# Where the first stores of batched V go, and in which order the first segment adds up its output

## The chip, the cores and the metric

The kernel runs on one core of a Trainium2 chip. The metric is device time in microseconds (us) of one execution. The core's engines have these names in the profile: PE is TensorE (matmuls; its weight loads are PEld), DVE is VectorE, ACT is ScalarE, POOL is GpSimd, SP is SyncE, which mostly starts transfers. L712 is line 712 of the kernel in question, so the same statement has another number in another kernel: the output sums (Wo) are L701 in the kernel before, L712 in the changed one, and L714 in experiments that add two lines.

## The reference, cut to what matters

```python
for s in range(n_seg):                      # 64 segments of 32 rows
    xs = x[:, s*32:(s+1)*32, :]
    h = concatenate([mem, xs])              # 8 memory rows + 32 rows, 512 wide
    q, k, v = h @ Wq, h @ Wk, h @ Wv        # 32 heads of 128
    p = softmax(mask(q @ k.T * scale))
    o = (p @ v) @ Wo                        # back to 512
    mem = o[:, :8, :]                       # what the next segment needs
    outs.append(o[:, 8:, :])
# ... then a residual, a layer norm and a gated feed-forward part
```

The segments are a chain: segment 1 cannot project its memory rows before segment 0's output has been summed over all heads. At the start the four weight matrices (4 MB each) also have to come in, and Wo is the last of them.

## The kernel before

The last 8 of each segment's 32 rows are taken out of the chain: their Q, K and V are computed in batches of 16 segments (128 rows), ahead of the segments that use them; this is "batched V". Batch ck = 0 covers segments 0 to 15. Its V tiles n = 0 to 7 are scaled into SBUF and go to device memory by GpSimd; the first four tiles of ck = 1 follow on the SyncE queue behind Wo:

```python
def vx_evac(ck, n, bank, eng="act", q="sp"):
    if ck == 1 and n < 4:
        t, tok = (hbuf, xo)[n // 2][:, n % 2, :], ...
    elif ck == 0:
        t, tok = part[:, n, :], ...
    else:
        t, tok = Vs[:, 0, :], [("Vs", 0)]
    # ... PSUM -> t on ACT or DVE
    if q is not None:
        em.add(q, lambda e: e.dma_start(dst, ...), reads=tok, writes=[("vext", ck, n)], dma=True)
    return lambda: sp(lambda e: e.dma_start(dst, ...), ...)
# ...
for n in range(8):
    # ...
    start_v(0, n)                 # store at once, by GpSimd
    if n % 2 == 1:
        start_v(1, n // 2)        # its store is kept in `stores`
# ...
for hq in range(4):
    load_wo(hq)                   # 4 x 1 MB
# ... batched K; V loads of segments 0 and 1
for f in stores:
    f()
```

At the end of each segment, Wo is summed for one half of the 512 columns, then for the other. The first half's memory columns (`mem_out`) are what the next segment's first projection waits for:

```python
Wo(WOQ, OB, 0, OC)                # 32 matmuls, first half, all quarters of Wo
part_evac(s, OB, 0, OC)           # ACT
Wo(WOQ[:6], OB2, OC, D)           # 24 of the second half
if s + 1 < NSEG:
    mem_out(s, 0)                 # PE, then the copy into hT on DVE
    mask_dve()
Wo(WOQ[6:], OB2, OC, D)           # the last 8
```

The softmax here doesn't subtract the row's maximum and nothing guards it: scores larger than these inputs give would overflow.

Of the kernel before, what the change touches and what calls it, by code (L numbers as in the profile page):

```python
# [178 lines left out]
def fast_path(nc, st, keep, A_x, A_mem0, A_Wq, A_Wk, A_Wv, A_Wo, A_seg_len, B_w_in, B_w_sp, B_b_sp, B_w_out, out):  # L179
    S = A_x.shape[1]  # L180
    D = A_x.shape[2]
# [13 lines left out]
    CK = 16  # L195
# [9 lines left out]
    em = Emitter(n_dma_sems=40)  # L205

    def sb(name, shape, dt):
        return st.enter_context(nc.sbuf_tensor("f_" + name, shape, dt))
# [11 lines left out]
    w_o = region(3 * WSZ, WSZ).rearrange("p (h d) -> p h d", h=H)  # L220
# [14 lines left out]
    NVX = 3  # L235
    Vx = sb("Vx", [128, NVX, 2, 128], BF)
    Vs = sb("Vs", [128, 2, 512], BF)
# [3 lines left out]
    part = sb("part", [128, 8, 512], BF)  # L241
    partx = sb("partx", [128, 512], BF)
    xn = sb("xn", [128, 2, 512], BF)
    hbuf = sb("hbuf", [128, 2, 512], BF)
    xo = sb("xo", [128, 2, 512], BF)
    wst = sb("wst", [128, RB, 64], BF)
    ident = sb("ident", [128, 128], BF)
    mask = sb("mask", [128, 448], BF)
    ones = sb("ones", [128, 128], BF)
# [20 lines left out]
    wT_d = nc.dram_tensor("wT_d", [S // 64, 128, RB, 64], BF, kind="Internal").ap()  # L270

    ps = st.enter_context(nc.psum_tensor("f_ps", [128, 8, 512], F32))
# [8 lines left out]
    def sp(fn, **k):  # L281
        return em.add("sp", fn, dma=True, **k)
# [217 lines left out]
                   reads=[("hTe", ck % 3, dc // 2), ("W", 2, n // 2)], writes=[PB(bank)])  # L500

    def vx_evac(ck, n, bank, eng="act", q="sp"):
        if ck == 1 and n < 4:
            t, tok = (hbuf, xo)[n // 2][:, n % 2, :], [(("h", "xo")[n // 2], n % 2)]
        elif ck == 0:
            t, tok = part[:, n, :], [("part", n, 0), ("part", n, 1)]
        else:
            t, tok = Vs[:, 0, :], [("Vs", 0)]
        if eng == "act":
            act(lambda e: e.activation(out=t, in_=ps[:, bank, :], func=ACT.Copy, scale=VSC), reads=[PB(bank)], writes=tok)  # L510
        else:
            dve(lambda e: e.tensor_scalar(out=t, in0=ps[:, bank, :], scalar1=VSC, scalar2=None, op0=ALU.mult), reads=[PB(bank)], writes=tok)
        dst = vext_d[ck, n // 4, 2 * (n % 4):2 * (n % 4) + 2, :, :].rearrange("g p f -> p g f")
        if q is not None:
            em.add(q, lambda e: e.dma_start(dst, t.rearrange("p (g f) -> p g f", g=2)), reads=tok, writes=[("vext", ck, n)], dma=True)
        return lambda: sp(lambda e: e.dma_start(dst, t.rearrange("p (g f) -> p g f", g=2)), reads=tok, writes=[("vext", ck, n)])

    def load_vx(s, q="sp"):
        i = s % CK
        for b in range(2):  # L520
            src = vext_d[s // CK, b, :, 8 * i:8 * i + 8, :].rearrange("g k (r e) -> g (k r) e", r=2)
            em.add(q, lambda e, b=b, src=src: e.dma_start(Vx[:, s % NVX, b, :], src),
                   reads=[("vext", s // CK, n) for n in range(4 * b, 4 * b + 4)], writes=[("Vx", s % NVX, b)], dma=True)



# [6 lines left out]
    OB = 2  # L533
# [3 lines left out]
    OB2 = 6  # L537
    FBK = 7
    OC = 256
# [151 lines left out]
    cTh = cT[:].rearrange("p c (b g q) -> p (c b g) q", b=2, q=40)  # L691


    WOQ = ((0, 0), (2, 0), (0, 1), (2, 1), (1, 0), (3, 0), (1, 1), (3, 1))

    def Wo(cbs, bank, d0, d1):
        for c, b in cbs:
            for g in range(4):
                h = 16 * b + 4 * c + g
                i = 8 * c + 4 * b + g  # L700
                pe(lambda e, h=h, g=g, i=i, b=b, c=c: e.matmul(  # L701
                    ps[32 * g:32 * g + 32, bank, 0:d1 - d0], lhsT=cTh[:, i, 8:40], rhs=w_o[:, h, d0:d1], start=((c, b) == WOQ[0]),
                    stop=((c, b) == WOQ[-1]), tile_position=(0, 32 * g)),
                    reads=[("cT", c, b), ("Wo", h // 8)], writes=[PB(bank)])

    def cTx_copy(s):
# [5 lines left out]
    def part_evac(s, bank, d0, d1):  # L712
        act(lambda e: e.activation(out=part[:, s % 8, d0:d1], in_=ps[:, bank, 0:d1 - d0], func=ACT.Copy), reads=[PB(bank)],  # L713
            writes=[("part", s % 8, d0 // OC)])  # L714
# [77 lines left out]
    NWT = S // 64  # L792

    def wT_piece(i):
        sp(lambda e: e.dma_start_transpose(out=wst[:, :, :], in_=B_w_sp[i * 64:(i + 1) * 64, :]), writes=["wst"])
        sp(lambda e: e.dma_start(wT_d[i], wst[:, :, :]), reads=["wst"], writes=[("wTd", i)])


    act(lambda e: e.preload_act_table_set("natural_log_exp_and_others"))
# [31 lines left out]
    def start_group(mm, ev, *a):  # L831
        cnt = scnt[0]
        scnt[0] += 1
        bk = ebank[cnt % 4]
        mm(*a, bk)
        return ev(*a, bk, "act" if cnt % 2 == 0 else "dve")

    stores = []

    def start_v(ck, n):  # L840
        if ck == 0:
            start_group(vx_mm, lambda *a: vx_evac(*a, q="pool"), ck, n)
        else:
            stores.append(start_group(vx_mm, lambda *a: vx_evac(*a, q=None), ck, n))

    for i in range(2, 8):
        for ck in range(2):
# [65 lines left out]
    for s in range(NSEG):  # L913
# [113 lines left out]
        cT_evac(3, "dve", (1,))  # L1027
        for f in xs[4:]:
            f()
        Wo(WOQ, OB, 0, OC)  # L1030
        part_evac(s, OB, 0, OC)
        Wo(WOQ[:6], OB2, OC, D)
        if s + 1 < NSEG:
            mem_out(s, 0)
            mask_dve()
        Wo(WOQ[6:], OB2, OC, D)
        cTx_copy(s)
        part_evac(s, OB2, OC, D)
        if j4 == 0 and 2 <= rb + 2 < RB:
# [127 lines left out]
    for rb in range(RB):  # L1167
# [19 lines left out]
        if rb in (2, 3):  # L1187
            r, j, bank = RB - 4 + rb, (rb - 1) % 2, zbank()
# [842 lines left out]
```

## Time and profile before

| | kernel before |
|---|---|
| median of 3 runs | 855.34 us (854.96 to 855.81) |
| TensorE busy | 837.4 us of the profiled span, 98% |
| batched V by GpSimd (queue q0) | 1.05 MB, 8 stores |
| Wk waits on TensorE | 0.21 and 1.36 us |
| gap ahead of the first Wo | 2.55 us, until 55.19 |
| first projection of segment 0 and of segment 1 | 44.20 and 58.30 us |

The lines behind these rows stand in the prediction. One more view belongs here, the transfers by issuing queue. The columns are: destination and source, queue, number of transfers, KB each, and the median us from issue to landing where known. The GpSimd queue (POOLq) moves eight whole tiles, and the SyncE queue (SPq) the four kept ones.

```profile
vext_d<-f_part POOLq DMA_DIRECT2D x8, 128.0 KB, 5.9
...
vext_d<-f_hbuf SPq DMA_DIRECT2D x2, 128.0 KB
vext_d<-f_xo SPq DMA_DIRECT2D x2, 128.0 KB
```

### The profile page before, as it was taken

What the parts mean: (1) busy time and instruction counts of PE and PEld (TensorE: products, weight loads), DVE (VectorE), ACT (ScalarE), POOL (GpSimd) and SP (SyncE); (2) the same over time, 40 slices, a digit from 0 to 9 for tenths busy, and PEclk for the clock granted to TensorE, in tenths of its full rate; (3) what the DMA queues carried; (4) which work ended last, traced back from release to release, by engine and by line L of the source; (5) the groups of instructions that cost most, each with busy time, mean ns of one, the idle gap of its engine ahead of it and who ended that gap; (6) DMA issues with size and microseconds to landing.
All of it is one profiled execution on the core that took longest, in us unless ns stands there. A gap on an engine that the chain in (4) does not pass through costs nothing.

```text
span 854.1 us, 45974 instructions
## 1 busy us (share of the span) xinstructions
PE 837.4 (98%) x22504; PEld 442.0 (52%) x19432; DVE 513.3 (60%) x1318; ACT 472.5 (55%) x1367; POOL 169.1 (20%) x425
## 2 busy tenths in 40 slices
PE   8889999999999999999999999999999999999997
PEld 8545555555555555555555555555555444444443
DVE  3446666666766666666767666666666554453443
ACT  3446666766667676667666676766676655400000
POOL 7312212122212122221222121222111232100000
PEclk9999999999999999999999999999999999999999
DMA  9972222222332222322223423243321780032101
GB/s 319 391 238 60 68 68 34 60 67 65 72 97 57 49 65 42 75 38 60 59 72 73 94 59 78 73 80 76 65 48 49 206 266 1 1 111 97 39 13 41
DMA packets 112922, 75.27 MB, mean 88 GB/s; under 512 B 70728, under 2 KB 98512, under 8 KB 112720
## 3 DMA queue, kind: packets, MB, share of 16 engines
q1 hardware_dynamic: 111504, 70.88, 30.8%
q8 instruction: 166, 2.72, 1.4%
q0 software_dynamic: 384, 1.05, 0.3%
q10 hardware_dynamic: 832, 0.33, 0.2%
q14 instruction: 36, 0.29, 0.1%
HBM read 39.46 MB, written 20.58 MB: 70 GB/s over the span
## 4 chain that ended last, share of the span: by engine, by line
PE 92%; SPq 3%; DMA 2%; DVE 1%; ACT 1%; issue 1%; ACTq 0%
PE f_ps L289 33%; PE f_ps L701 14%; PE f_ps L290 12%; PE f_ps L1146 11%; PE f_ps L751 3%; PE f_ps L666 3%; PE f_ps L1220 3%; PE f_ps L1108 3%; PE f_ps L1139 3%; SPq L329 2%; PE f_ps L498 2%; DMA f_arena<-in_A_Wk_dram 2%; PE f_ps L595 1%; PE f_ps L615 1%; PE f_ps L672 1%
## 5 line engine op out<-in xcount | busy, mean ns | idle before, releaser
L289 PE MATMUL f_ps<-f_arena,f_hT 128*32 128x512 bf16 (+1 forms) x5632 | 360.6, 331 | 0.2
L289 PEld LDWEIGHTS f_ps<-f_arena,f_hT 128*32 128x32 bf16 x5632 | 134.7, 96 | 160.2 <-issue 69.3
L290 PE MATMUL f_ps<-f_arena,f_hT 128*32 128x512 bf16 (+1 forms) x2560 | 189.7, 315 | 0.0
L559 ACT ACTIVATE f_Tst<-f_ps 128x512 bf16<-128x512 f32 (+1 forms) x320 | 149.6, 510 | 57.8 <-PE f_ps L289 54.1
L701 PE MATMUL f_ps<-f_arena,f_cT 128*32 128x256 bf16 x4096 | 132.4, 275 | 1.5 <-ACT f_cT L686 0.8
L638 POOL TENSOR_TENSOR f_E_sb<-f_R_sb,f_E_sb 128x64 bf16<-128x64 f32 x128 | 57.1, 446 | 362.0 <-ACT f_R_sb L630 362.0
L567 DVE STREAM_TRANSPOSE f_QT<-f_Tst 128x256 uint32<-128x256 uint32 x128 | 57.0, 446 | 95.4 <-ACT f_Tst L559 95.4
L701 PEld LDWEIGHTS f_ps<-f_arena,f_cT 128*32 128x32 bf16 x4096 | 92.0, 95 | 38.0 <-ACT f_cT L686 21.7
L1146 PE MATMUL f_ps<-f_arena 128*128 128x512 bf16 x448 | 100.6, 379 | 0.0
L688 DVE TENSOR_SCALAR f_cT<-f_ps 128x160 bf16<-128x160 f32 x256 | 65.1, 316 | 34.5 <-PE f_ps L672 34.5
L713 ACT ACTIVATE f_part<-f_ps 128x256 bf16<-128x256 f32 x128 | 49.2, 384 | 60.7 <-PE f_ps L701 57.1
L658 DVE TENSOR_SCALAR f_V_sb<-f_ps 128x512 bf16<-128x512 f32 (+1 forms) x128 | 71.0, 555 | 13.7 <-PE f_ps L289 13.7
L686 ACT ACTIVATE f_cT<-f_ps 128x160 bf16<-128x160 f32 x256 | 57.1, 309 | 35.5 <-PE f_ps L672 35.5
L1146 PEld LDWEIGHTS f_ps<-f_arena 128*128 128x128 bf16 x448 | 43.8, 98 | 52.7
L567 DVE STREAM_TRANSPOSE f_KT<-f_Tst 128x128 uint32<-128x128 uint32 (+1 forms) x192 | 65.8, 356 | 2.7
L626 ACT ACTIVATE f_R_sb<-f_ps 128x160 f32<-128x160 f32 x128 | 39.0, 305 | 34.8 <-PE f_ps L290 31.5
L634 DVE TENSOR_TENSOR f_E_sb<-f_R_sb,f_E_sb 128x160 bf16<-128x160 f32 x128 | 41.7, 326 | 23.4 <-ACT f_R_sb L630 23.4
L1152 DVE TENSOR_TENSOR f_arena<-f_ps,f_arena 128x512 f32<-128x512 f32 x28 | 19.3, 690 | 54.4 <-PE f_ps L1146 52.4
L289 PE MATMUL f_ps<-f_arena,f_hTe 128*32 128x512 bf16 x640 | 48.9, 382 | 0.0
L608 ACT ACTIVATE f_E_sb<-f_ps 128x224 bf16<-128x224 f32 x128 | 45.8, 358 | 0.0
L751 PE MATMUL f_ps<-f_arena,f_cTx 128*32 128x512 bf16 x512 | 44.2, 379 | 0.0
L630 ACT ACTIVATE f_R_sb<-f_R_sb 128x160 f32<-128x160 f32 x128 | 42.6, 333 | 2.0
(117 smaller groups left out, 1026.6 us busy)
## 6 DMA issues: line engine op xcount, KB each, us to landing
wT_d<-f_wst SPq DMA_DIRECT2D x32, 256.0 KB
f_arena<-wT_d SPq DMA_DIRECT2D x32, 256.0 KB
f_arena<-in_A_Wv_dram SPq DMA_DIRECT2D x4, 1024.0 KB
f_arena<-in_A_Wk_dram SPq DMA_DIRECT2D x4, 1024.0 KB
f_arena<-in_A_Wo_dram SPq DMA_DIRECT2D x4, 1024.0 KB
f_Vx<-vext_d SPq DMA_DIRECT2D x124, 32.0 KB
f_arena<-in_A_Wq_dram SPq DMA_DIRECT2D x3, 1024.0 KB
vext_d<-f_Vs SPq DMA_DIRECT2D x20, 128.0 KB
```

What stands on the lines that cost most here:

```text
L289: return e.matmul(out, lhsT=lhsT, rhs=rhs, start=start, stop=stop, skip_group_check=True, tile_position=pos)
L290: return e.add_instruction(mybir.InstMatmult(name=nc.get_next_instruction_name(), engine=mybir.EngineType.PE, ins=[e.lower_ap(rhs), e.lowe ...
L559: act(lambda e: e.activation(out=st_.rearrange("p (hp i r) -> p hp i r", i=32, r=2), in_=ps[:, bank, 0:64 * np_].rearrange("p (hp r i) -> ...
L567: dve(lambda e: e.transpose(out=dst, in_=src), reads=tok, writes=[(nm, b, k) for k in halves(b, p0, np_)])
L638: pool(lambda e: e.tensor_tensor(out=ev, in0=rv, in1=ev, op=ALU.mult), reads=[("R", b), ("Ex", b)], writes=[("Ex", b)])
L658: dve(lambda e: e.tensor_scalar(out=dst, in0=src, scalar1=VSC, scalar2=None, op0=ALU.mult), reads=[PB(bank)], writes=tok)
L686: act(lambda e: e.activation(out=dst, in_=src, func=ACT.Copy, scale=UNSC), reads=[PB(PVB[c])], writes=tok)
L688: dve(lambda e: e.tensor_scalar(out=dst, in0=src, scalar1=UNSC, scalar2=None, op0=ALU.mult), reads=[PB(PVB[c])], writes=tok)
L701: pe(lambda e, h=h, g=g, i=i, b=b, c=c: e.matmul(ps[32 * g:32 * g + 32, bank, 0:d1 - d0], lhsT=cTh[:, i, 8:40], rhs=w_o[:, h, d0:d1], star ...
L713: act(lambda e: e.activation(out=part[:, s % 8, d0:d1], in_=ps[:, bank, 0:d1 - d0], func=ACT.Copy), reads=[PB(bank)], writes=[("part", s % ...
L751: pe(lambda e, h=h, g=g, i=8 * qr + bg: e.matmul(ps[32 * g:32 * g + 32, WXB, :], lhsT=cTx[:, rb % 2, i, :], rhs=w_o[:, h, :], start=(i < 4 ...
L1146: pe(lambda e: e.matmul(ps[:, bank, 0:TB], lhsT=z2[:, sc, fb * 128:(fb + 1) * 128], rhs=wTb[tb % 2][:, :, sc, :], start=(sc == 0), stop=(s ...
```

## The change

The intent: only segments 0 to 3 need their batched V soon, and it lies in partitions 0 to 31 of each tile. So GpSimd stores that quarter alone, and SyncE stores the rest behind Wo. Less traffic goes ahead of Wk and Wo (queue q0 moves 0.26 MB, before 1.05). The rest must wait longer in SBUF, so the tiles move to buffers that are free for that long: two of them to `Vs`. Second, segment 0 sums Wo in pieces over both halves, in the order in which Wo's quarters land, so that TensorE has work before the last quarter is there.

```diff
     def vx_evac(ck, n, bank, eng="act", q="sp"):
-        if ck == 1 and n < 4:
-            t, tok = (hbuf, xo)[n // 2][:, n % 2, :], ...
-        elif ck == 0:
-            t, tok = part[:, n, :], ...
+        if ck == 0:
+            t = (hbuf, xo, Vs, wst2)[n // 2][:, n % 2, :]
+            tok = [(("h", "xo", "Vs", "wst")[n // 2], n % 2)]
+        elif ck == 1 and n < 4:
+            i = (n + 3) % 4 + 4
+            t, tok = part[:, i, :], ...
...
+        if q == "sp":
+            store(q, 0, 128)
+        elif q == "pool":
+            store(q, 0, 32)
+        return lambda: store("sp", 32 if q == "pool" else 0, 128)
...
-        Wo(WOQ, OB, 0, OC)
-        part_evac(s, OB, 0, OC)
-        Wo(WOQ[:6], OB2, OC, D)
+        if s == 0:
+            q0 = [(c, b) for b in range(2) for c in range(4)]
+            for i, d0 in ((0, 0), (1, 0), (0, OC), (1, OC), (2, 0), (2, OC), (3, 0)):
+                Wo(q0[2 * i:2 * i + 2], OB2 if d0 else OB, d0, d0 + OC, q0[0], q0[-1])
+            part_evac(s, OB, 0, OC)
+        else:
+            ...                   # as before
         if s + 1 < NSEG:
             mem_out(s, 0)
             mask_dve()
-        Wo(WOQ[6:], OB2, OC, D)
+        if s == 0:
+            Wo(q0[6:], OB2, OC, D, q0[0], q0[-1])
+        else:
+            Wo(WOQ[6:], OB2, OC, D)
```

Cut: the passing of `first` and `last` through Wo, the tokens of `wst`, and the split of the `vext` tokens in two, so that the loads of segments 0 to 3 wait for the early stores alone.

More of the change, by code (lines that the diff above doesn't have):

```diff
@@ L246, in fast_path @@
     wst = sb("wst", [128, RB, 64], BF)
+    wst2 = wst[:].rearrange("p r c -> p (r c)").rearrange("p (j f) -> p j f", j=2)
     ident = sb("ident", [128, 128], BF)
@@ L502, in vx_evac @@
     def vx_evac(ck, n, bank, eng="act", q="sp"):
-        if ck == 1 and n < 4:
-            t, tok = (hbuf, xo)[n // 2][:, n % 2, :], [(("h", "xo")[n // 2], n % 2)]
-        elif ck == 0:
-            t, tok = part[:, n, :], [("part", n, 0), ("part", n, 1)]
+        if ck == 0:
[3 more added lines that the diff above has]
+            i = (n + 3) % 4 + 4
+            t, tok = part[:, i, :], [("part", i, 0), ("part", i, 1)]
         else:
@@ L513, in vx_evac, with store @@
         dst = vext_d[ck, n // 4, 2 * (n % 4):2 * (n % 4) + 2, :, :].rearrange("g p f -> p g f")
-        if q is not None:
-            em.add(q, lambda e: e.dma_start(dst, t.rearrange("p (g f) -> p g f", g=2)), reads=tok, writes=[("vext", ck, n)], dma=True)
-        return lambda: sp(lambda e: e.dma_start(dst, t.rearrange("p (g f) -> p g f", g=2)), reads=tok, writes=[("vext", ck, n)])
+        src = t.rearrange("p (g f) -> p g f", g=2)
+        def store(q, p0, p1):
+            em.add(q, lambda e: e.dma_start(dst[p0:p1], src[p0:p1]), reads=tok, dma=True,
+                   writes=[("vext", ck, n, i) for i in range(2) if p0 <= 32 * i < p1])
+        if q == "sp":
[3 more added lines that the diff above has]
+        return lambda: store("sp", 32 if q == "pool" else 0, 128)
     def load_vx(s, q="sp"):
@@ L522, in load_vx @@
             em.add(q, lambda e, b=b, src=src: e.dma_start(Vx[:, s % NVX, b, :], src),
-                   reads=[("vext", s // CK, n) for n in range(4 * b, 4 * b + 4)], writes=[("Vx", s % NVX, b)], dma=True)
+                   reads=[("vext", s // CK, n, int(s % CK > 3)) for n in range(4 * b, 4 * b + 4)], writes=[("Vx", s % NVX, b)], dma=True)
     QKP = ((0, 0, 8, 0, 0), (0, 0, 8, 1, 1), (1, 0, 8, 0, 6), (1, 0, 4, 1, 7), (1, 4, 4, 1, 2))
@@ L694, in fast_path, with Wo @@
     WOQ = ((0, 0), (2, 0), (0, 1), (2, 1), (1, 0), (3, 0), (1, 1), (3, 1))
-    def Wo(cbs, bank, d0, d1):
+    def Wo(cbs, bank, d0, d1, first=WOQ[0], last=WOQ[-1]):
         for c, b in cbs:
@@ L701, in Wo @@
                 pe(lambda e, h=h, g=g, i=i, b=b, c=c: e.matmul(
-                    ps[32 * g:32 * g + 32, bank, 0:d1 - d0], lhsT=cTh[:, i, 8:40], rhs=w_o[:, h, d0:d1], start=((c, b) == WOQ[0]),
-                    stop=((c, b) == WOQ[-1]), tile_position=(0, 32 * g)),
+                    ps[32 * g:32 * g + 32, bank, 0:d1 - d0], lhsT=cTh[:, i, 8:40], rhs=w_o[:, h, d0:d1], start=((c, b) == first),
+                    stop=((c, b) == last), tile_position=(0, 32 * g)),
                     reads=[("cT", c, b), ("Wo", h // 8)], writes=[PB(bank)])
@@ L794, in wT_piece @@
     def wT_piece(i):
-        sp(lambda e: e.dma_start_transpose(out=wst[:, :, :], in_=B_w_sp[i * 64:(i + 1) * 64, :]), writes=["wst"])
-        sp(lambda e: e.dma_start(wT_d[i], wst[:, :, :]), reads=["wst"], writes=[("wTd", i)])
+        tok = [("wst", 0), ("wst", 1)]
+        sp(lambda e: e.dma_start_transpose(out=wst[:, :, :], in_=B_w_sp[i * 64:(i + 1) * 64, :]), writes=tok)
+        sp(lambda e: e.dma_start(wT_d[i], wst[:, :, :]), reads=tok, writes=[("wTd", i)])
     act(lambda e: e.preload_act_table_set("natural_log_exp_and_others"))
@@ L840, in start_v @@
     def start_v(ck, n):
-        if ck == 0:
-            start_group(vx_mm, lambda *a: vx_evac(*a, q="pool"), ck, n)
-        else:
-            stores.append(start_group(vx_mm, lambda *a: vx_evac(*a, q=None), ck, n))
+        stores.append(start_group(vx_mm, lambda *a: vx_evac(*a, q=None if ck else "pool"), ck, n))
     for i in range(2, 8):
@@ L1029, in fast_path @@
             f()
-        Wo(WOQ, OB, 0, OC)
-        part_evac(s, OB, 0, OC)
-        Wo(WOQ[:6], OB2, OC, D)
+        if s == 0:
[4 more added lines that the diff above has]
+        else:
+            Wo(WOQ, OB, 0, OC)
+            part_evac(s, OB, 0, OC)
+            Wo(WOQ[:6], OB2, OC, D)
         if s + 1 < NSEG:
```

## The prediction

> **What bounds the kernel now.** I read the page first, then the timeline of 0 to 60 us, the waits, and the windows with the granted clock. One row says that the kernel as a whole is bound by TensorE:
>
> ```profile
> PE 837.4 (98%) x22504; PEld 442.0 (52%) x19432; DVE 513.3 (60%) x1318; ACT 472.5 (55%) x1367; POOL 169.1 (20%) x425
> q8 instruction: 166, 2.72, 1.4%
> q0 software_dynamic: 384, 1.05, 0.3%
> ```
>
> The change keeps every matmul (3,896 rows on PE before and after in the instruction orders), so it can only touch the 2% in which PE does nothing, and of that only the start, because the code of segments 1 to 63 is as it was. There PE is not the bound; the transfers are. The mean busy share of the DMA engines is nine tenths in all slices up to about 54 us (0 to 120 us in slices of 3 us):
>
> ```profile
> DMA  1999999999999999994252032035023443001354
> ```
>
> Three places of the timeline carry the argument: Wk arriving late, the first segment's Wo, and the next segment's start.
>
> ```profile
> 38.93 1.96 PE L463 MATMUL f_ps<-f_hTe,f_arena 128*128 128x128 bf16 x32 [0.21 <-DMA f_arena<-in_A_Wk_dram]
> 42.25 2.02 PE L463 MATMUL f_ps<-f_hTe,f_arena 128*128 128x128 bf16 x33 [1.36 <-DMA f_arena<-in_A_Wk_dram]
> ...
> 44.20 0.40 PE L289 MATMUL f_ps<-f_arena,f_hT 128*32 128x512 bf16 x4
> ...
> 55.19 0.38 PE L498 MATMUL f_ps<-f_arena,f_hTe 128*32 128x512 bf16 x1 [2.55 <-issue]
> 55.20 2.08 PEld L701 LDWEIGHTS f_ps<-f_arena,f_cT 128*32 128x32 bf16 x55 [3.05 <-issue]
> 55.20 2.56 PE L701 MATMUL f_ps<-f_arena,f_cT 128*32 128x256 bf16 x55
> 55.61 0.69 DVE L512 TENSOR_SCALAR f_Vs<-f_ps 128x512 bf16<-128x512 f32 x1 [2.40 <-PE f_ps L498]
> ...
> 58.08 0.17 DVE L728 CAST f_hT<-f_ps 128x16 bf16<-128x16 f32 x1 [1.78 <-PE f_ps L722]
> ...
> 58.30 0.62 PE L289 MATMUL f_ps<-f_arena,f_hT 128*32 128x512 bf16 x4
> ```
>
> The reader sees PE stand 0.21 + 1.36 = 1.57 us for Wk, then 2.55 us ahead of Wo (L701). Segment 0 takes from 44.20 to 58.30, 14.1 us; segment 2 takes 9.73 (68.51 to 78.24). From the batched V matmuls after PV to the next segment it is 52.03 to 58.30 = 6.27 us, in segment 1 65.98 to 68.51 = 2.53: 3.74 us too long. The windows show why it is more than the wait:
>
> ```profile
> core 0: us, PE busy (x) PEld busy (x) DVE busy (x) ACT busy (x) POOL busy (x), PEclk, DMA share, GB/s
> 55.00:56.00 1.00, 0.81 (x31) 0.80 (x34) 0.39 (x1) 0.00 (x0) 0.00 (x0) 1.00 0.30 99
> 56.00:57.00 1.00, 1.00 (x32) 0.94 (x24) 0.30 (x1) 0.27 (x1) 0.00 (x0) 0.53 0.10 30
> 57.00:58.00 1.00, 1.00 (x29) 0.87 (x22) 0.00 (x0) 0.11 (x1) 0.00 (x0) 0.50 0.46 131
> 58.00:59.00 1.00, 1.00 (x14) 0.19 (x8) 0.93 (x3) 0.39 (x1) 0.00 (x0) 0.50 0.15 33
> 59.00:60.00 1.00, 1.00 (x28) 0.40 (x20) 0.56 (x2) 0.18 (x1) 0.23 (x2) 0.77 0.20 47
> ```
>
> After the gap PE works at half clock until about 59.5. The next segment's projections take 58.30 to 62.36 = 4.06 us instead of 68.51 to 72.08 = 3.57: another 0.49. What the Wo gap costs is 3.74 + 0.49 = 4.2 us; with the Wk waits, 5.8 us is all there is to win, 0.7% of the time.
>
> **Why PE stood for 2.55 us.** The semaphore increments in the trace give the landings of the four Wo quarters: 45.13, 48.12, 51.22 and 55.21. Before, the first half needs all four within 13 matmuls, so Wo's last quarter would hold PE until 55.21. But the first of the two rows that ends the gap is a batched V matmul that waits for nothing; it is labelled "issue", and the 16 KB instruction packet of the q8 row ran only from 52.62 to 53.82, the one before from 43.39 to 44.54, some 460 PE instructions earlier. So I think two things end within 0.02 us of each other: late Wo and late instructions.
>
> [...] Wk quarters and the last of Wv land 2.71 us apart (26.50 to 29.21) while there are no stores, and 3.20, 3.27, 3.20 and 3.32 apart while GpSimd's V stores run. [...] Here half clock lasted about 3.4 us (56.06 to 59.5), after a gap of under 3 us.
>
> **The change part by part.**
> *V stores.* Before, GpSimd stores 8 tiles of 128 KB, 1.05 MB, among the weights. Now it stores partitions 0 to 31 alone, 32 KB each; 8 stores of 96 KB follow on the SyncE queue behind Wo, among the four of 128 KB that were there. The 1.05 MB took 2.3% of 16 engines over 120 us = 2.76 us; three quarters are 2.07. From the landings: four intervals of 12.99 us against 4 x 2.71 = 10.84, so 2.15, three quarters 1.6. I take 1.6 to 2.1 us earlier for Wk's and Wo's last quarters.
> *Wk.* Last quarter at 40.1 to 40.6 instead of 42.20. PE, without waits, would be ready at 42.25 - 1.57 = 40.68. Both waits go: 1.57 us, first segment at 42.63. The four V loads on the ScalarE queue, which hold back the first eviction (46.71), follow PE's evictions and move along.
> *Wo.* Last quarter at 53.1 to 53.6. PE comes to Wo at about 51.0. By pieces it has 48 of 64 matmuls, at 27 ns each (1.57 us for 56), that need only three quarters: 1.3 us, then it waits until 53.1 to 53.6. Eight matmuls later (0.22) the first half is done, 0.39 us eviction, memory columns: with the hand-overs of segment 1 the next segment could start near 54.7 to 55.0, 3.4 us earlier. But the first half is now ended with 8 matmuls left beside its eviction instead of 32, perhaps 0.5 us exposed, which is in this figure.
> *A new wait.* VectorE's eviction of batched V in segment 0 writes the Vs buffer (55.61 above). Before it waits for PE alone. In the new instruction order it waits also for a DMA: the seventh SyncE store (tile 4 of the first batch lies in Vs now). It stands on VectorE ahead of the copy of the memory columns (58.08), on which the next segment waits. The four stores behind Wo landed at 55.58, 55.92, 56.25 and 56.61, 0.34 us each. Seven stores, five of 96 KB: 5 x 0.255 + 2 x 0.34 = 1.96 us after Wo. So 53.1 to 53.6 + 1.96 = 55.1 to 55.6; eviction 0.69, copy 0.17, hand-overs 0.1: next segment at 56.0 to 56.5 instead of 58.30, **1.8 to 2.3 us** earlier. This, not Wo, is what I expect to set the end.
> *Clock.* The 0.49 us comes back if the clock stays up. PE has 0.9 to 1.3 us idle for Wo and then about 1.5 us for VectorE, broken by short work; I give half clock an even chance, at about 1 us. It nearly cancels.
> Sum: 855.3 - (1.8 to 2.3) - 0.49 + 0.5 = 853.0 to 853.5; I say **853.2 us**.
>
> **The rivals.**
> *A: the new wait is hidden.* If the stores are faster or SyncE gets to them sooner, the next segment starts at 54.7 to 55.0 at full clock: 3.4 + 0.49 = 3.9 us, 851.4. For it: Wo's landing of 55.21 has one engine's increment 0.8 us behind the other fifteen (54.41), which a different mix may take away. Against it: seven stores in one queue behind Wo.
> *B: instructions stay late.* The request for that block comes 1.57 us earlier, and the engines are just as full. PE then resumes at about 53.6, all 56 matmuls come after it, and half clock follows as before: next segment at about 57, gain 1.3 us, 854.0. For it: the gap's label[...].
> *C: transfers only change places.* The bytes ahead of the x load for later rows are the same, so it lands at 57 as before (56.89), while VectorE asks for it 2 us sooner. If that, the Vs wait and half clock add up, the gain is under 0.6 us: 854.8.
> *D: the gain is the V store alone*, with no profit from the Wo order: 1.6 us, 853.7.
>
> **Range and chances.** The ends are A with some luck (851.2) and C (854.9, still inside the runs of before, 854.96 to 855.81, almost). All there is to win is 5.8 us = 0.7%, and nothing that could lose 17 us: within 2% is all but certain.
>
> **What would show it.** Right: no wait for Wk on PE ahead of L463; the segment's first projection near 42.6; VectorE's eviction into Vs waiting for a DMA store, at 55 to 56; the second segment's first projection at 56 to 56.5. Wrong: the Vs eviction ends its wait on PE (A); a gap "issue" of over 2 us again ahead of Wo, with half clock behind it (B); a wait for the x load on VectorE (C); or a time over 855, which would mean that stores behind Wo delay something in segments 1 to 4 that I hold to be far off the path.

The sum came to 853.0 to 853.5 us. Its "+ 0.5" is half of "about 1 us", the even chance of half clock. Both figures are my estimate and no measured rate: the one profile behind them has a single stretch of half clock between 4.85 and 854.77 us, from 56.05 to 59.47.

## The result, and the profile after

The changed kernel took 855.37 us (median of 4 runs, 854.37 to 857.22), the kernel before in the same rounds 855.58 us (4 runs, 854.96 to 857.48). Ratios here are the mean time of one kernel's fast runs over that of the other's of the same rounds (in the experiments the profiled run lies outside the rounds), so they are not quite the ratio of the medians: 0.9996, 95% interval 0.9973 to 1.002. 855.37 is above the predicted range of 851.2 to 854.9.

The transfers of the changed kernel show the intended move: a quarter of each tile by GpSimd, three quarters by SyncE (shown for four of the eight tiles, in `Vs` and `wst`).

```profile
vext_d<-f_Vs SPq DMA_DIRECT2D x2, 96.0 KB
vext_d<-f_wst SPq DMA_DIRECT2D x2, 96.0 KB
...
vext_d<-f_Vs POOLq DMA_DIRECT2D x2, 32.0 KB, 5.5
vext_d<-f_wst POOLq DMA_DIRECT2D x2, 32.0 KB, 5.1
```

The timeline of the changed kernel, same columns as before (start, us busy, engine, line, operation, tiles, count, and in brackets the idle time before it with what ended it):

```profile
37.83 5.02 PE L464 MATMUL f_ps<-f_hTe,f_arena 128*128 128x128 bf16 x87
...
42.78 0.40 PE L290 MATMUL f_ps<-f_arena,f_hT 128*32 128x512 bf16 x4
...
53.38 0.59 PE L499 MATMUL f_ps<-f_arena,f_hTe 128*32 128x512 bf16 x1 [2.17 <-issue]
...
55.85 0.69 DVE L515 TENSOR_SCALAR f_Vs<-f_ps 128x512 bf16<-128x512 f32 x1 [4.07 <-DMA vext_d<-f_Vs]
...
56.78 0.38 ACT L724 ACTIVATE f_part<-f_ps 128x256 bf16<-128x256 f32 x1 [5.19 <-PE f_ps L712]
...
57.50 0.17 DVE L739 CAST f_hT<-f_ps 128x16 bf16<-128x16 f32 x1 [0.95 <-PE f_ps L733]
57.72 0.10 PEld L290 LDWEIGHTS f_ps<-f_arena,f_hT 128*32 128x32 bf16 x4 [0.33 <-DVE f_hT L739]
57.72 0.40 PE L290 MATMUL f_ps<-f_arena,f_hT 128*32 128x512 bf16 x4
```

The batched K matmuls (L464) run as one group of 87 without a wait, where two groups waited for Wk; segment 0 begins at 42.78 instead of 44.20, 1.42 us earlier. But the gap "issue" is back at the same instruction, the last batched V matmul, 2.17 us long. The first half of Wo is now evicted at 56.78 (ACT L724) where it was 56.73. VectorE's eviction into `Vs` did wait for a store, as predicted (55.85), but it was done before the copy into `hT` could start (57.50), and that copy waited 0.95 us for TensorE. So of 1.42 us won for segment 0, 58.30 - 57.72 = 0.58 us reached segment 1.

The windows of the changed kernel say why the first half took from 53.38 to 56.78 (columns: window, its length, the five engines' busy time and instructions, granted clock, DMA share, GB/s):

```profile
53.00:54.00 1.00, 0.62 (x14) 0.50 (x15) 0.00 (x0) 0.00 (x0) 0.00 (x0) 0.50 1.03 304
54.00:55.00 1.00, 1.00 (x24) 0.88 (x20) 0.00 (x0) 0.00 (x0) 0.00 (x0) 0.50 0.96 276
55.00:56.00 1.00, 1.00 (x28) 0.85 (x23) 0.14 (x1) 0.00 (x0) 0.00 (x0) 0.50 0.70 200
56.00:57.00 1.00, 0.75 (x14) 0.37 (x6) 0.55 (x1) 0.21 (x1) 0.00 (x0) 0.80 0.59 176
```

TensorE does 24 to 28 matmuls per us at clock 0.50, and all 56 of the pieces stand ahead of the eviction; in the old order only 32 do. At the start of segment 2's score exponentials the changed kernel was 1.07 us ahead (71.57 against 72.64), and still so in segment 6 (110.49 against 111.58). Later, single segments of either kernel took 0.3 to 0.6 us longer than the rest, at different places, and this profile, the slowest of the four runs (857.22 us), lost the lead in them. Such jitter is why I compare landmarks at the start and not ends of single profiles.

### The profile page after: what moved, and what is told of

The parts are those of the page before. It is cut to its first block, busy times and chain, and to the rows that moved or that the text cites. A ratio compares the mean times of both kernels' runs of the same rounds, so it can differ in the third digit from the quotient of the medians.

```text
span 855.5 us, 45989 instructions
## 1 busy us (share of the span) xinstructions
PE 837.9 (98%) x22504; PEld 442.5 (52%) x19432; DVE 513.8 (60%) x1318; ACT 472.1 (55%) x1367; POOL 167.2 (20%) x425
## 3 DMA queue, kind: packets, MB, share of 16 engines
q8 instruction: 166, 2.72, 1.3%
## 4 chain that ended last, share of the span: by engine, by line
PE 94%; DVE 1%; ACT 1%; DMA 1%; issue 1%; ACTq 0%; SPq 0%
PE f_ps L290 32%; PE f_ps L712 14%; PE f_ps L291 12%; PE f_ps L1164 11%; PE f_ps L499 3%; PE f_ps L762 3%; PE f_ps L677 3%; PE f_ps L1238 3%; PE f_ps L1126 3%; PE f_ps L1157 3%; PE f_ps L464 2%; PE f_ps L606 1%; PE f_ps L626 1%; DMA f_arena<-in_A_Wq_dram 1%; PE f_ps L683 1%
## 5 line engine op out<-in xcount | busy, mean ns | idle before, releaser
L570 ACT ACTIVATE f_Tst<-f_ps 128x512 bf16<-128x512 f32 (+1 forms) x320 | 149.7, 510 | 58.4 <-PE f_ps L290 54.7
L724 ACT ACTIVATE f_part<-f_ps 128x256 bf16<-128x256 f32 x128 | 49.1, 383 | 61.7 <-PE f_ps L712 58.2
```

The lines of the kernel that those rows point to most:

```text
L570: act(lambda e: e.activation(out=st_.rearrange("p (hp i r) -> p hp i r", i=32, r=2), in_=ps[:, bank, 0:64 * np_].rearrange("p (hp r i) -> ...
L724: act(lambda e: e.activation(out=part[:, s % 8, d0:d1], in_=ps[:, bank, 0:d1 - d0], func=ACT.Copy), reads=[PB(bank)], writes=[("part", s % ...
```

## The experiments

**The theory after the result.** The transfers moved as predicted. What kept the time is the instruction supply, and the half clock behind its gap: TensorE runs out of instructions just ahead of Wo, in both kernels (2.55 and 2.17 us). When they come, everything that the pieces should have done early comes late, and often at half clock (in six of the nine unshifted profiles with that gap, in the table below). The instructions themselves arrive in packets of 16 KB each (queue q8 of the page, 2.72 MB in 166 packets in either kernel); their times come from the trace's records of that queue. The packet before the gap ran from 51.00 to 52.08, and TensorE went on 1.30 us after its end; before the change it was 52.62 to 53.82, and 1.37 us. **Rivals:** the store wait on VectorE (`Vs`), the late x load, or an order by pieces that is worth nothing in itself.

Landmarks of all runs, in us. "Gap" is the wait labelled "issue" next to the first Wo, with the time at which TensorE went on; "half clock" is a granted clock near 0.50 between 53 and 60. Times are medians where there are several runs. The ratio is to the kernel before, which had 4 runs beside the changed kernel and 11 in each of the later sets. The state of a kernel that ran once is unknown; of these only the landmarks are used.

| run | gap, TensorE goes on | half clock | segment 1 begins | time | ratio [95%] |
|---|---|---|---|---|---|
| before (first profile) | 2.55, 55.19 | yes | 58.30 | 855.34 | |
| e5_before_again | 0.90, 54.57 | no | 56.84 | 853.64 (1 run) | |
| after | 2.17, 53.38 | yes | 57.72 | 855.37 | 0.9996 [0.9973, 1.002] |
| e6_after_again | 1.54, 53.09 | yes | 57.51 | 854.58 | 0.9984 [0.9971, 0.9997] |
| e1_store_only | 1.30, 53.05 | no | 56.36 | 856.1 | 0.9997 [0.9982, 1.0012] |
| e2_wo_only | 1.96, 55.38 | no | 58.26 | 857.52 | 1.0017 [1.0, 1.0034] |
| e3_tile4_elsewhere | 1.68, 53.34 | yes | 57.46 | 858.98 (1 run) | |
| e4_stream_shifted | 1.77, 54.39 (in Wo) | no | 56.55 | 855.9 (1 run) | |
| e7_three_mends | 2.39, 53.89 | yes | 57.32 | 852.86 | 0.9957 [0.9943, 0.9971] |
| e8_three_mends_shifted | none ahead of Wo; 0.84, 56.06, behind its first half | no | 56.49 | 851.7 | 0.9947 [0.9935, 0.9958] |
| e12_best_again (as e8) | none | no | 54.99 | 853.65 | 0.9955 [0.9942, 0.9968] |
| e9_pieces_mends_shifted | none | no | 55.43 | 854.54 | 0.9965 [0.9947, 0.9983] |
| e11_after_shifted | none ahead of Wo; 0.19, 54.43, behind | from 56.8 | 56.09 | 855.9 | 0.9978 [0.9958, 0.9998] |
| e15 (as e11) | none ahead of Wo; 0.34, 54.69, behind | no | 56.05 | 853.34 | 0.9967 [0.9944, 0.999] |
| e13_before_shifted | none ahead of Wo; 0.40, 57.01, behind | no | 57.44 | 855.06 | 0.998 [0.9958, 1.0002] |
| e10_wo_held_back | 2.23, 53.89 | yes | 59.80 | 859.43 (1 run) | |
| e14_wo_held_longer | none | yes | 63.53 | 865.33 (1 run) | |

All of them gave correct results. The four sets ran on different chips, and their times are not compared: the kernel before itself had medians from 856.27 to 857.28 us in them.

### One part alone: the stores, or the order

e1 keeps the stores of the change and takes back the order of Wo:

```diff
-        if s == 0:          # both places: order by pieces
+        if False:
```

> The new V stores with the old order of the first segment's Wo. Theory I (late instructions, half clock, and the pieces put the first half behind 56 matmuls): first projection of segment 0 at 42.8 as in the changed kernel, the gap labelled issue still ends near 53.4, and because the first half is done after 32 matmuls the next segment starts at 56.6 to 57.0, earlier than the 57.72 of the changed kernel; time about 1.5 us under before. Rival W (Wo's last quarter is what holds PE, so the pieces are worth having): the next segment starts later than 57.72, and the time is not under that of the changed kernel.

e2 is the kernel before with the order by pieces alone:

```diff
+        if s == 0:
+            q0 = [(c, b) for b in range(2) for c in range(4)]
+            for i, d0 in ((0, 0), (1, 0), (0, OC), (1, OC), (2, 0), (2, OC), (3, 0)):
+                Wo(q0[2 * i:2 * i + 2], OB2 if d0 else OB, d0, d0 + OC, q0[0], q0[-1])
+            part_evac(s, OB, 0, OC)
...                           # cut: the rest, as in the change
```

> The old V stores with the new order of the first segment's Wo. Theory I: first projection of segment 0 at 44.2 as before, gap labelled issue until about 55.2, and the next segment starts later than the 58.30 of before, at 59.0 to 59.6; time 0.7 to 1.3 us over before. Rival W: PE no longer stands for Wo's last quarter, the next segment starts at 57.5 or earlier; time under before.

Neither part won time: 0.9997 and 1.0017. For e1 that is a miss, since 1.5 us had been expected; e2's start of segment 1, 58.26, lies between my theory (59.0 to 59.6) and its rival (57.5 or earlier). The timeline of the kernel with the stores alone is the clearest view of the store wait:

```profile
53.05 0.38 PE L499 MATMUL f_ps<-f_arena,f_hTe 128*32 128x512 bf16 x1 [1.30 <-issue]
54.34 0.38 ACT L724 ACTIVATE f_part<-f_ps 128x256 bf16<-128x256 f32 x1 [2.21 <-PE f_ps L712]
...
55.53 0.69 DVE L515 TENSOR_SCALAR f_Vs<-f_ps 128x512 bf16<-128x512 f32 x1 [3.21 <-DMA vext_d<-f_Vs]
56.14 0.17 DVE L739 CAST f_hT<-f_ps 128x16 bf16<-128x16 f32 x1
...
56.36 0.40 PE L290 MATMUL f_ps<-f_arena,f_hT 128*32 128x512 bf16 x4 [1.13 <-DVE f_hT L739]
...
58.73 0.70 DVE L379 BATCH_NORM_STATS2 f_st<-f_xn 128x6 f32<-128x512 bf16 x1 [1.89 <-DMA f_xn<-in_A_x_dram]
```

Here the clock stayed up and the old order evicted the first half at 54.34, yet segment 1 began only at 56.36. The memory columns were ready on TensorE near 55.0, but VectorE stood at the `Vs` eviction, which waited for a store until 55.53, and TensorE waited 1.13 us for VectorE. This is the predicted new wait, at the predicted hour (55.1 to 55.6). Behind it comes the x load, now late on VectorE (1.89 us) because SyncE is still issuing stores (it comes to the load at 56.18, in the kernel before at 50.38); TensorE's scores then wait 0.25 us for the transposes behind it. In e2, from the end of the gap to segment 1 it is 58.26 - 55.38 = 2.88 us; in e5, the old order at the same full clock, 56.84 - 54.57 = 2.27:

```profile
55.38 1.90 PE L701 MATMUL f_ps<-f_arena,f_cT 128*32 128x256 bf16 x56
57.32 0.38 ACT L713 ACTIVATE f_part<-f_ps 128x256 bf16<-128x256 f32 x1 [3.52 <-PE f_ps L701]
...
58.26 0.40 PE L289 MATMUL f_ps<-f_arena,f_hT 128*32 128x512 bf16 x4
```

So when instructions are late, the pieces cost 0.61 us, because the first half waits for 56 matmuls and not 32.

### Without the store wait

e3 takes away what VectorE waits for: tile 4 goes to a buffer that is free at that time.

```diff
         if ck == 0:
             t = (hbuf, xo, Vs, wst2)[n // 2][:, n % 2, :]
             ...
+            if n == 4:
+                t, tok = partx[:, :], ["partx"]
```

> The changed kernel with V tile 4 of the first batch in a buffer that nobody uses until segment 6, so that VectorE's eviction of batched V in segment 0 waits for no store. Theory I: the eviction ends its wait on PE, at about 54.0 instead of 55.85, but the next segment starts at 57.7 as in the changed kernel (within 0.2), since it waits for PE's own first half. Rival V (the store wait sets the end, as predicted): the next segment starts at 56.9 or earlier.

```profile
53.35 3.12 PE L714 MATMUL f_ps<-f_arena,f_cT 128*32 128x256 bf16 x56
53.76 0.69 DVE L517 TENSOR_SCALAR f_Vs<-f_ps 128x512 bf16<-128x512 f32 x1 [1.53 <-PE f_ps L499]
...
57.46 0.40 PE L290 MATMUL f_ps<-f_arena,f_hT 128*32 128x512 bf16 x4
```

The wait is gone (the eviction starts at 53.76, after TensorE), but segment 1 begins at 57.46, 0.26 us before the changed kernel's first profile and 0.05 before its second (e6). In the changed kernel the store wait was therefore not what set the end; the late and slow first half was.

### The position in the instruction stream

If the instruction packets are the limit, it must matter where in the stream one of them ends. e4 makes the warm-up at the start 43 weight loads shorter. Its 44 matmuls now also write 32 rows and not 128; nothing behind the warm-up changes:

```diff
-    for _ in range(44):
-        pe(lambda e: e.matmul(ps[:, 1, 0:128], lhsT=onesrc[:, 0:128], rhs=onesrc[:, 0:128], ...
+    for i in range(44):
+        pe(lambda e, i=i: mm(e, i > 0, ps[0:32, 1, 0:128], onesrc[:, 0:32], onesrc[:, 0:128], ...
```

> The changed kernel with 43 weight loads fewer in the warm-up (same matmul count), which shifts every later PE instruction by 43 places against the 16 KB blocks. Theory I: the gap labelled issue moves by 43 PE rows: the last batched V matmul and about 21 Wo matmuls run first, near 51 us, and the gap of 2 us or so comes among the Wo matmuls, ending some 1.3 us after the instruction packet ends. Rival W or any wait that belongs to the instruction itself: the gap stays at the last batched V matmul ahead of Wo.

The gap moved with the stream, by the 43 records (one batched V matmul, 21 matmuls of Wo and 21 of their weight loads). In the timeline of e4 all batched V matmuls and 21 of Wo run first, and the wait labelled "issue" stands between two Wo matmuls, where no data is missing:

```profile
51.51 1.11 PE L712 MATMUL f_ps<-f_arena,f_cT 128*32 128x256 bf16 x21
54.39 1.16 PE L712 MATMUL f_ps<-f_arena,f_cT 128*32 128x256 bf16 x35 [1.77 <-issue]
```

The instruction packet there ended at 52.97, 1.42 us before TensorE went on. Segment 1 began at 56.55. That is 1.17 us earlier than in the changed kernel, although the instructions came 1.01 us later than there (54.39 against 53.38). Two things differ: 21 matmuls were done before the gap, and the clock stayed up. The clock is the larger one by its size: the 56 matmuls took 3.37 us in the changed kernel, mostly at half clock (granted 0.50), and 1.90 in e2 at full clock (1.00).

e11 shifts the other way and further, by 128 TensorE instructions (64 more matmuls, each with its weight load), with about as many columns in the warm-up (5,616 and 5,632):

```diff
-    for _ in range(44):
-        pe(lambda e: e.matmul(ps[:, 1, 0:128], ..., rhs=onesrc[:, 0:128], ...
+    for _ in range(108):
+        pe(lambda e: e.matmul(ps[:, 1, 0:52], ..., rhs=onesrc[:, 0:52], ...
```

> The changed kernel with its stream shifted by 128 TensorE instructions (108 warm-up matmuls of 52 columns instead of 44 of 128) and nothing else. My theory: the loss at the first Wo is late instructions; the gap ahead of Wo goes or moves, the first half is ready early, and the next segment is set by VectorE's eviction of batched V behind its store: first projection at 56.3 to 56.6 instead of 57.5 to 57.7, no half clock there, time about 1 us under the changed kernel's, ratio to the kernel before about 0.997. Rival, that the position in the instruction stream does not matter: next segment at 57.5 or later, ratio as the changed kernel's, 0.998 to 1.000.

```profile
51.40 2.14 PE L712 MATMUL f_ps<-f_arena,f_cT 128*32 128x256 bf16 x56
...
55.26 0.69 DVE L515 TENSOR_SCALAR f_Vs<-f_ps 128x512 bf16<-128x512 f32 x1 [3.13 <-DMA vext_d<-f_Vs]
...
56.09 0.40 PE L290 MATMUL f_ps<-f_arena,f_hT 128*32 128x512 bf16 x4 [1.26 <-DVE f_hT L739]
```

With instructions on time TensorE runs all 56 Wo matmuls in one go from 51.40, and the prediction's picture comes true: the store lands, VectorE evicts at 55.26 and copies, and segment 1 begins at 56.09; predicted was 56.0 to 56.5. The clock, however, fell to half at 56.8 in this profile, after 1.26 us of idle TensorE, which I had not expected, and the x load held VectorE for 1.88 us, so the start of segment 2's exponentials (71.92) was no earlier than in the changed kernel (71.57). In time, 0.9978 is not told apart from the changed kernel's 0.9984; the 1 us that I had expected is not shown.

### What the change is worth when instructions are on time

The worth of the change without late instructions was still open. e13 is the kernel before with the same shift of 128; e15 is e11 again in the same rounds.

> The kernel before with its stream shifted by 128 TensorE instructions (108 warm-up matmuls of 52 columns instead of 44 of 128). My theory, that the prediction's sum holds where instructions are not late: TensorE waits for Wo's last quarter (DMA), which lands near 55.2, the next segment's first projection is at 57.0 to 57.6, and this kernel is 1.0 to 2.5 us slower than the changed kernel with the same shift. Rival, that transfers are not the limit before either and the change is worth nothing even then: next segment at 56.0 to 56.6 and the two shifted kernels within 0.7 us.

> The changed kernel with the same shift, once more, for the direct comparison with the kernel before with that shift. My theory: next segment's first projection at 56.0 to 56.6, after a wait for VectorE behind its store, and 1.0 to 2.5 us faster than the other. Rival: the two within 0.7 us.

In the timeline of e13 TensorE waits for Wo's last quarter, a transfer, with eleven of the matmuls done, which is what the kernel before was meant to be bound by:

```profile
55.09 1.48 PE L701 MATMUL f_ps<-f_arena,f_cT 128*32 128x256 bf16 x45 [0.61 <-DMA f_arena<-in_A_Wo_dram]
...
55.96 0.38 ACT L713 ACTIVATE f_part<-f_ps 128x256 bf16<-128x256 f32 x1 [1.45 <-PE f_ps L701]
...
57.01 0.17 PE L722 MATMUL f_ps<-f_G_sb,f_part 128*32 128x8 bf16 x1 [0.40 <-issue]
...
57.44 0.40 PE L289 MATMUL f_ps<-f_arena,f_hT 128*32 128x512 bf16 x4
```

Segment 1 begins at 57.44 against 56.05 in e15, 1.39 us. But not even e13 has all its instructions on time: the last of the eight `mem_out` matmuls (L722) comes late, 1.63 us after the end of a packet (55.38). From the start of the eviction to segment 1 it is 57.44 - 55.96 = 1.48 us here, and 54.99 - 54.03 = 0.96 in e12, which has no such gap. So about 0.5 of the 1.39 us are late instructions, and I estimate the worth of the change itself at 0.9 us. (e15 has the same gap, 0.34 us, but there VectorE is later still.) In time the medians are 1.72 us apart (855.06 and 853.34), the means 1.05 (854.95 and 853.90), with six runs each that overlap; the two traces show a gain, the times are only in agreement with it.

### The kernel before, and the changed one, once more

Both ran again unchanged.

> The kernel before, once more, for a second profile. [...] this profile may show none: then the gap labelled issue still ends within 0.5 us of 55.2, and the next segment starts at 57.3 to 57.6 instead of 58.30, with the score exponential of segment 2 at about 71.2 instead of 72.64. If half clock belongs to the gap as such: 58.3 and 72.6 again.

> The changed kernel, once more. Without half clock the next segment would start at about 56.6 (set by VectorE's wait for the store of the Vs buffer), with it at 57.5 to 57.9 as in the first profile. The gap labelled issue stays at the last batched V matmul, 1.5 to 2.5 us. Time: 0 to 1 us under before, the interval of the ratio holding 1.

In the first of the two, "none" stands for no half clock.

e5 shows that the base of my prediction was one draw of several:

```profile
54.57 0.38 PE L498 MATMUL f_ps<-f_arena,f_hTe 128*32 128x512 bf16 x1 [0.90 <-issue]
...
56.84 0.40 PE L289 MATMUL f_ps<-f_arena,f_hT 128*32 128x512 bf16 x4
```

The same program has a gap of 0.90 us here and not 2.55, no half clock, and begins segment 1 at 56.84 and not 58.30, earlier than I had expected (57.3 to 57.6). Of the 1.65 us between the two gaps, 1.03 is TensorE coming to the place later, as segment 0 began at 45.23 and not 44.20. e6 looks like the changed kernel's first profile (57.51; half clock), and its time is 0.16% under the kernel before, with an interval that leaves out 1 by little (I had expected 1 inside it). The mean clock of the other runs doesn't tell how often half clock comes at this place: in e5 and e12 it is 0.999 only because the clock is at half in the last 2.5 and 1.8 us of the execution, and no half clock is near Wo (1.00 in all windows from 50 to 60 us). The 3.4 us of half clock in the two profiles of the changed kernel (52.99 to 56.41 in the first) take 1.7 of 855 us, 0.002, off the mean. Three of its nine runs show 0.999, too much for a stretch of that length; the other six (0.997 and 0.998) can have had it.

### Why the instructions are late

e10 and e14 are slower on purpose. Both hold back Wo's third and fourth quarter and the twelve stores, so that the DMA engines are idle when TensorE's next instruction packet is wanted: e10 until the first segment's K projections are done, e14 until its last PV matmul.

```diff
-    for hq in range(4):
+    for hq in range(2):
         load_wo(hq)
...
-    for f in stores:
-        f()
...
+            for hq in range(2, 4):
+                load_wo(hq, [lastop["k"]])     # e14: [last PV matmul], after PV_half(s, 1)
+            for f in stores:
+                f()
```

> The changed kernel with the third and fourth quarter of Wo and the twelve stores issued only after the first segment's K projections (near 46 us), so that the DMA engines are nearly idle when TensorE's next block of instructions is asked for. Slower at this point on purpose: Wo's last quarter lands later and TensorE waits for it. My theory, that the block is late because its packets stand behind full DMA engines: no wait labelled issue of over 0.5 us at the last batched V matmuls ahead of Wo; [...] the wait ahead of Wo is labelled with the DMA of Wo instead. Rival, that the block is late for a reason of its own, whatever the transfers do: a gap labelled issue of 1.5 to 2.5 us stays at the same instruction.

> The changed kernel with Wo's third and fourth quarter and the stores issued only after the last PV matmul of the first segment, near 51 us, so that the DMA engines are nearly idle from about 46.5 to 51 us. Theory, that the instruction block is late because its packets stand behind full DMA engines: the packet that came at 50.6 to 52.6 in all runs without a shift now starts by 49.5 and there is no gap labelled issue of over 0.5 us at the last batched V matmuls; TensorE waits for Wo by DMA instead, longer than before. Rival, that the block is late whatever the transfers do: the packet starts at 51 or later and a gap of 1.2 to 2.5 us labelled issue stays at the same instruction.

e10 was a miss: the gap stayed at 2.23 us. But its engines were idle only from 47 to 48 us (9 GB/s; 73 GB/s in the half us before) and full again from 49 (300 GB/s), so it did not decide. e14 did. Its windows from 48 and 50 us, then its timeline:

```profile
48.00:50.00 2.00, 2.00 (x91) 1.18 (x71) 1.46 (x4) 1.38 (x7) 0.44 (x1) 1.00 0.06 12
50.00:52.00 2.00, 1.81 (x68) 0.99 (x72) 1.34 (x5) 1.21 (x6) 0.84 (x2) 1.00 0.01 2
```

```profile
50.77 0.74 PE L499 MATMUL f_ps<-f_arena,f_hTe 128*32 128x512 bf16 x8
51.22 1.34 PE L712 MATMUL f_ps<-f_arena,f_cT 128*32 128x256 bf16 x32
57.54 1.05 PE L712 MATMUL f_ps<-f_arena,f_cT 128*32 128x256 bf16 x16 [4.98 <-DMA f_arena<-in_A_Wo_dram]
```

With the DMA share at 0.06 and 0.01, the packet started at 48.25 instead of 50.59 to 52.88 in the unshifted runs with full engines (DMA share 1.07 to 1.13 from 50 to 52 us); counted from segment 0's first projection, 5.32 us instead of 6.86 to 8.42. All eight batched V matmuls and 32 of Wo run without a gap, and the wait is for Wo's data, as it must be here. So the packet came earlier, and no gap was left, where there were few data transfers; that instruction packets stand behind them rests on this one profile. In e10 the packet came at 51.48, after the traffic was back.

### A version that beats both

e7 puts together what e1 and e3 showed: the new stores, the old order, tile 4 in a buffer of its own, and the x load issued ahead of the stores. e8 adds the shift by 128; e12 is e8 again; e9 is e8 with the order by pieces.

```diff
+            if n == 4:
+                t, tok = partx[:, :], ["partx"]
...
+    load_x(2, 0)
     for f in stores:
         f()
...
-        if j4 == 0 and 2 <= rb + 2 < RB:
+        if j4 == 0 and 2 < rb + 2 < RB:
             load_x(rb + 2, 0)
...
-        if s == 0:          # order by pieces, twice; e9 keeps it
+        if False:
```

> The new V stores, the old order of Wo, V tile 4 in a buffer that nobody needs, and the x load for later rows issued ahead of the stores. If the store wait and the x load are all that the change added in waits: VectorE's eviction of batched V and its batch-norm statistics wait for no DMA, the next segment starts 2.1 to 2.3 us after PE leaves the gap labelled issue, near 55.3 without half clock, score exponential of segment 2 near 69.4; time 1.5 to 2 us under before. If something else holds segment 1 (a weight load of Wo, the queue of SyncE): later than 56.

> As the run with three mends, with 108 warm-up matmuls of 52 columns instead of 44 of 128 (the same columns), which puts every later PE instruction 128 places on against the 16 KB blocks[...]. Theory I: the place at which PE runs out moves 128 rows back, to the score or V matmuls of segment 0 near 48.5 us; the gap there is shorter or gone (0 to 2 us), none is left ahead of Wo, PE then stands at Wo for its last quarter until about 53.6; the next segment starts at about 55.5. If it is Wo and not instructions that holds PE in any case: no difference from the run without the shift in the segment's start.

> The changed kernel with its order of Wo by pieces, and with the three things that the best version so far (three mends, stream shifted by 128 instructions) has: tile 4 of batched V in a buffer of its own, the x load issued ahead of the stores, 128 more matmuls in the warm-up. My theory: once instructions are not late ahead of Wo, the pieces use the time in which the old order waits 1.8 us for Wo's last quarter; TensorE then waits for that quarter only with 8 + 8 matmuls left, until about 53.7, and the next segment's first projection starts at 55.0 to 55.6 instead of 56.49; time up to 1 us under that version's (its ratio to the kernel before was 0.9947), ratio about 0.994. Rival: the first half, which ends with 8 matmuls beside its eviction, and a later supply of instructions hold the end where it was; next segment at 56.3 or later, ratio 0.995 or above.

> The version with the old Wo order, three mends and the shifted stream once more, on the same chip and in the same rounds as the piece order, so that the two orders are compared directly. If it repeats: ratio 0.994 to 0.996 to the kernel before; next segment at 56.3 to 56.7 without half clock. If the earlier 0.9947 was luck of the start: 0.996 to 0.998, with a gap labelled issue somewhere between 50 and 56 us.

e7 took 852.86 us, e8 851.7, in rounds in which the kernel before took 856.27 and the changed kernel 854.58. e8 over the changed kernel is 851.84 / 854.66 = 0.9967 by their means, and e12 repeated the ratio to the kernel before, 0.9955 after 0.9947. How much of this the shift adds is not resolved: e7 had 0.9957 without it. The profiled run of e7 was its slowest (854.74 us; the fastest was 851.0), with a gap of 2.39 us and half clock. Its segment 1 began at 57.32 (expected near 55.3 without half clock), about as in the changed kernel, so this profile does not show where its gain comes from. e8's profile has the shortage of instructions at another place, not earlier, as I had expected, but behind the first half of Wo, as in e13:

```profile
54.57 0.39 ACT L726 ACTIVATE f_part<-f_ps 128x256 bf16<-128x256 f32 x1 [2.65 <-PE f_ps L714]
...
56.06 0.17 PE L735 MATMUL f_ps<-f_G_sb,f_part 128*32 128x8 bf16 x1 [0.84 <-issue]
...
56.49 0.40 PE L290 MATMUL f_ps<-f_arena,f_hT 128*32 128x512 bf16 x4
```

The shift moves the place at which instructions run out; it doesn't do away with it. In e12, the same program, the packet for that place ended at 52.98 and not at 54.52, nothing was late, and segment 1 began 1.5 us earlier (54.99; 56.3 to 56.7 had been expected). In e12's timeline TensorE waits ahead of the first half for Wo alone:

```profile
53.17 1.48 PE L714 MATMUL f_ps<-f_arena,f_cT 128*32 128x256 bf16 x45 [0.73 <-DMA f_arena<-in_A_Wo_dram]
```

e9 and e12 compare the two orders with no store wait, no late x load and no gap ahead of Wo. By pieces, segment 1 began at 55.43, in the old order at 54.99, after segment 0 had begun at 43.56 and 43.33; the means are 854.15 and 853.54 us. The pieces do away with the 0.73 us for Wo, but they put all 56 matmuls ahead of the eviction. I had expected them to win up to 1 us here. No gain is shown.

## Why the prediction was wrong

853.2 us was predicted, 855.37 measured. The predicted ratio, 853.2 / 855.3 = 0.9975, lies inside the first measured interval and at the edge of e6's, so the times alone would not refute it. The traces do: segment 1 gained 0.58 us from one profile to the other, not 1.8 to 2.3. And with the second profiles, 56.84 (e5) and 57.51 (e6), not even that is left: 58.30 and 56.84 before, 57.72 and 57.51 after.

**The V stores and Wk: right.** Both Wk waits went in this profile, and segment 0 began at 42.78 (predicted 42.63); five of the other twelve profiles with the new stores kept one wait, of 0.36 to 0.87 us. Wo's last quarter landed at 53.64 (53.1 to 53.6).

**The new wait on VectorE: right in kind and hour, not in its rank.** The `Vs` eviction waited for its store until 55.85 (predicted 55.1 to 55.6). That it sets the end was wrong in the changed kernel (e3: 0.26 us without it), and right where the first half is ready before the store has landed (e1 56.36, e11 56.09, e15 56.05; predicted 56.0 to 56.5).

**Wo: the step that failed.** "By pieces it has 48 of 64 matmuls ... that need only three quarters: 1.3 us" assumed that TensorE has the instructions. It didn't: it went on at 53.38, when Wo was nearly there, with all 56 still to do, and at half clock. This is rival B, which named the sign ("a gap 'issue' of over 2 us again ahead of Wo, with half clock behind it") and the time of resuming (53.6). I had set it aside with a reason that no trace had shown. What is measured: with few transfers the packet started at 48.25 (e14), and in the changed kernel, with the engines as full as before (a DMA share of 1.12 from 50 to 52 us in both), at 51.00. So where the prediction had 1.3 us of Wo done before the last quarter landed, the runs show none of it done, and 3.37 us for the 56 matmuls behind the gap. The half clock is the larger part of this: at full clock they took 1.90 us (e2), and segment 1 could have begun near 56.7, when VectorE had done with `Vs` (an estimate from 55.85 and the steps of e1). B's own figures were too kind: segment 1 at 57.72 and not about 57, since 56 matmuls at half clock are slower than I took them to be.

**The clock: the chance is not refuted, the cost was too low.** "An even chance" of half clock: both profiles of the changed kernel had it, and three of its nine runs cannot have had a stretch of that length. It was taken at about 1 us, and cost 1.5 on the 56 matmuls (3.37 against 1.90 us). What decides it is not shown: the profiles with gaps of 1.54 us (e6) and 2.17 us (after) have half clock, the one with 1.96 us (e2) has none.

**The base: wrong.** The 58.30 from which the gain was counted came from one profile. e5 puts the same event at 56.84. A predicted gain of 2 us cannot be read off a base that moves by 1.46 us between two runs of one kernel. From e13 to e15, without a gap ahead of Wo and at full clock, the gain is 1.39 us, of which about 0.9 us (the estimate above) does not come from late instructions: about half of the sum's first term.

**Rival C** (a late x load) is real, 1.66 to 1.89 us of VectorE in e1, e4, e11 and e15 and 0.80 in e3, but it doesn't show in the changed kernel, where everything ahead of it was later. **Rivals A and D**: A's hour for segment 1 (54.7 to 55.0) was reached only by e12, in which the store wait is taken away; and the stores alone gave 0.9997, no gain (D).

Open: why the packet's delay varies from run to run (in the kernel before it started 9.23 us after the packet ahead of it, and 7.62 in e5), how e7's gain divides among its three mends, and whether 1.05 us between e13 and e15 is more than chance.

## What to carry to other kernels

A wait labelled "issue" on the busiest engine, at an instruction whose data is ready, while the DMA engines are full, was here a sign of late instruction packets, so it is a reason to look at them: shift the stream by some dozens of cheap instructions and see whether the wait moves (in e4, by 43, it moved from the last batched V matmul to behind 21 matmuls of Wo). Then look where it went: in e8 and e13 it came back behind the first half. Splitting a sum so that it can start early puts more work ahead of its first result, and that was a loss of 0.61 us here (e2 against e5), where the start was held by something else. Before a gain of two microseconds is predicted, profile the kernel before more than once.
